# Attention for the next half woven into a feed-forward network: where TensorE's visits to the attention stand

## The chip, the cores and the metric

The kernel runs on one core of a Trainium2 chip. The metric is the device time of one execution in microseconds. The median of three runs of the kernel before is 941.1 us (940.64 to 941.63).

## What is computed

Attention over 8 batches, 8 heads, 576 positions and 64 dimensions, four heads with a plain window of 32 keys and four with 32 keys at a stride of 4; its result goes through a feed-forward network of 512 and 2048 with an exact GELU.

```python
def _attn_ref(q, k, v):
    scores = scale * np.matmul(q, k.transpose(0, 1, 3, 2))
    mask_plain = (rel >= 0) & (rel < window)
    mask_dil = (rel >= 0) & (rel < window * dilation) & (rel % dilation == 0)
    ...
    scores = np.where(masks[None, :, :, :], scores, -1000000000.0)
    scores = scores - np.max(scores, axis=-1, keepdims=True)
    attn = np.exp(scores)
    attn = attn / (np.sum(attn, axis=-1, keepdims=True) + 1e-09)
    return np.matmul(attn, v)

def _moe_ref(x, w_in, w_out):
    h = x @ w_in
    g = 0.5 * h * (1.0 + erf(h * inv_sqrt2))
    return g @ w_out
```

## The kernel before, in words

The 8 batches are cut into 16 halves of 288 positions, c = 0 to 15. For each half the heads form four pairs, p = 0 and 1 with the plain window and p = 2 and 3 with the dilated one. The network of a half takes 384 matrix products of 128 by 128 by 288 on TensorE: 16 hidden blocks of 12 each (`ffn_h`, L470) and four output blocks of 16 times 3 each (`ffn_o`, L484).

Halves 0 to 2 and the first two networks are ordered by a planner (`Plan`, up to L624). The change doesn't touch them. From the network of half 2 on (L667) the order is written out by hand: while TensorE works on the network of half c-1, the attention of half c is woven in. A step has a place, counted in units of 12 products: place f stands behind hidden block f, place 16 + 4d + f/4 behind the f-th part of output block d, and 32 is the start of the next network. `upto` (L661) emits each step when the loop comes to its place. Since every engine works through its instructions in the order in which they are emitted, a place sets where a step stands in the queue of each engine that it uses.

For half c, with places counted from the start of the network of half c-1:

- `load` (place -6, that is, place 26 of the network before): one DMA for each pair, issued on SP, for its queries and keys (`raw_qk`, L276). `all_v` (place 2): four DMAs for the values (L283).
- `scores_of` (A_SC, L629): TensorE multiplies queries with keys, 36 small products (64 rows by 32 columns, L328) for a plain pair, and for a dilated one 48 where c is even or 3, and 32 otherwise. Pairs 0 and 1 share one PSUM tile `ps_a`, pairs 2 and 3 the next; there are two such tiles in a ring that the later products share. Pairs 0 and 1 stand at place 3, pairs 2 and 3 at place 9.
- `lowest` (A_SC too, L340): VectorE adds the mask and finds the maximum, two or three steps a pair.
- `softmax` (places 16.25 to 17, L349): ScalarE's exponentials.
- `norm` and `turn` (places 18.5, 20, 21.5 and 23.25, L370 to L394): VectorE divides and transposes.
- `av_of` (A_X, L640): TensorE multiplies with v, as many small products (64 by 64, L429) as the scores had, into a `px_a` tile of the same ring. Pairs 0 and 1 stand at place 22.5, pairs 2 and 3 at place 27.
- `xout` (A_X too): ScalarE casts the product to the high part `xh` (L456), VectorE takes the low part `xl` (L459). Both feed the next network.

So TensorE leaves the network four times in a half for what is called a visit below: two for scores, two for products with v. There are 13 woven halves (3 to 15), so 52 visits. Around them stand the network's own steps: behind each hidden block a GELU and a cast on ScalarE (L474, L477) and a subtraction on VectorE (L479), behind each output block a copy on VectorE (L185) and a store that SP issues (L509).

Of the kernel before, what the change touches and what calls it, by code (L numbers as in the profile page):

```python
# [138 lines left out]
def attn_ffn(ctx: ExitStack, tc: tile.TileContext, qk_p, qk_d, qk_w, qk_r, v_p0, v_d0, v_p, v_d, w_in, w_out, outT):  # L139
# [129 lines left out]
    def load(s):  # L269

        yield {"DMA": 1.0 if s.plain else 1.2}
        if s.c < 2 or not s.plain:
            s.raw = wo.tile([P, 2 * DM], F32, tag="wo", name="raw_qk")
        else:
            s.raw = work.tile([P, HALF + KW], F32, tag="raw", name="raw_qk", bufs=5)
        nc.sync.dma_start(s.raw[:, 0:s.n], s.src)  # L276
# [8 lines left out]
    def all_v(c):  # L285

        v = work.tile([P, NPAIR, NU, 2, 2 * D], F32, tag="big", name="v_all", bufs=1)
        for s in xs[c]:
            s.v = v[:, s.p]
            yield from load_v(s)  # L290
# [4 lines left out]
    def rows_of(s, u):  # L295
        g = groups(s, u)
        return slice(32 * g[0], 32 * g[-1] + 32)
# [5 lines left out]
    def mask_of(s, u):  # L303
        k = ANY if s.c % 2 or u else PLAIN0 if s.plain else DILATED0
        return masks[rows_of(s, u), k]

    def scores(s, banks=None):

        yield {"PE": 0.75}
        if banks is None:  # L310
            s.sc = [ps_m.tile([P, 512], F32, tag="m", name="ps_sc")[:, 0:2 * KB * NU] for _ in range(2)]
        else:
            s.sc = [banks[:, h, s.p % 2 * 2 * KB * NU:(s.p % 2 + 1) * 2 * KB * NU] for h in range(2)]
        for u in range(s.nu):
            for r in groups(s, u):
                if s.across:
                    q0 = (4 * u + r if u < 2 else 8) * KB
                    k0 = HALF + q0
                elif s.split:

                    q0 = r * s.nq + u * KB
                    k0 = DIL * s.nq + r * s.nk + (u - (s.c % 2 == 0)) * KB
                else:
                    q0 = r * s.nq + u * KB
                    k0 = HALF + r * s.nk + u * KB
                for h in range(2):
                    x = s.raw[h * D:(h + 1) * D]
                    nc.tensor.matmul(s.sc[h][32 * r:32 * r + 32, u * 2 * KB:(u + 1) * 2 * KB], x[:, q0:q0 + 32],  # L328
                                     x[:, k0:k0 + 2 * KB], start=True, stop=True)

    def lowest(s, u):

        yield {"DVE": 0.28}
        if u == 0:
            s.sm = work.tile([P, 2 * NU, 2 * KB], F32, tag="sm", name="sm", bufs=5)
            s.st = work.tile([P, 2, 2 * NU], F32, tag="st", name="st", bufs=5)
        cols, rs = slice(u * 2 * KB, (u + 1) * 2 * KB), rows_of(s, u)
        for h in range(2):
            i = 2 * u + h
            nc.vector.tensor_tensor_reduce(  # L340
                out=s.sm[rs, i], in0=s.sc[h][rs, cols], in1=mask_of(s, u), scale=-SCALE,
                scalar=3.0e38, op0=ALU.add, op1=ALU.min, accum_out=s.st[rs, 0, i:i + 1])

    def softmax(s, u):
        yield {"ACT/exp": 0.66}
        for i in (2 * u, 2 * u + 1):
            rs = rows_of(s, u)
            t = s.sm[rs, i]
            nc.scalar.activation(t, t, AF.Exp, bias=s.st[rs, 0, i:i + 1], scale=-1.0, accum_out=s.st[rs, 1, i:i + 1])  # L349
# [16 lines left out]
    def norm(s):  # L366
        for rs, u0, u1 in parts(s):
            t, st = s.sm[rs, 2 * u0:2 * u1], s.st[rs, 1, 2 * u0:2 * u1]
            yield {"DVE": 0.07}
            nc.vector.tensor_scalar_add(st, st, EPS)  # L370
            yield {"DVE": 0.1}
            nc.vector.reciprocal(st, st)
            if s.c in (1, 2):
                yield {"Pool": 2.2}
                for i in range(2 * NU):
                    nc.gpsimd.tensor_scalar(t[:, i], t[:, i], st[:, i:i + 1], 1.0, op0=ALU.mult, op1=ALU.mult)  # L376
                continue
            yield {"DVE": 0.47}
            nc.vector.tensor_mul(t, t, st.unsqueeze(2).broadcast_to((rs.stop - rs.start, 2 * (u1 - u0), 2 * KB)))  # L379

    def turn(s):

        s.t = work.tile([P, 2 * NU, 2, KB], F32, tag="sm", name="turned", bufs=5)
        for rs, u0, u1 in parts(s):
            yield {"DVE": 0.5}
            i = slice(2 * u0, 2 * u1)
            nc.vector.transpose(s.t[rs, i].rearrange("p i j b -> p (i j b)"), s.sm[rs, i].rearrange("p i k -> p (i k)"))  # L389
            if s.c >= 2:  # L390
                for r in groups(s, u0):
                    yield {"DVE": 0.3}
                    to, j = r ^ 1, 1 - r % 2
                    nc.vector.transpose(s.t[32 * to:32 * to + 32, i, r % 2],  # L394
                                        s.sm[32 * r:32 * r + 32, i, j * KB:(j + 1) * KB])
# [37 lines left out]
    def xout(s):  # L433
        for i, (px, r0, r1) in enumerate(s.px):
            yield {"ACT": 0.46 if len(s.px) == 1 else 0.34}
            if i == 0:
                if s.c == 1:
                    s.x = s.of["x"][:, s.p, 0], s.of["x"][:, s.p, 1]
                else:
                    s.x = tuple(xpool.tile([P, HALF], F32R, tag=n, name=n) for n in ("xh", "xl"))  # L440
            if s.across:
                two = [x[:, 0:8 * KB].rearrange("p (u r b) -> p r u b", u=2, r=4) for x in s.x]
                put = [(px[:, :, 0:2 * KB].rearrange("p r (u b) -> p r u b", u=2), two),
                       (px[:, s.nine, 2 * KB:], [x[:, 8 * KB:] for x in s.x])]
            elif s.split:
                xs_ = [x.rearrange("p (i r) -> p r i", r=DIL) for x in s.x]
                if s.c % 2:
                    put = [(s.kept, [x[:, :, 0:QD - QR] for x in xs_]), (px, [x[:, :, QD - QR:] for x in xs_])]
                else:
                    put = [(px[:, :, 0:QD], xs_)]  # L450
                    nc.scalar.copy(s.kept, px[:, :, QD:])
            else:
                put = [(px, [x.rearrange("p (r i) -> p r i" if s.plain else "p (i r) -> p r i", r=s.nr)[:, r0:r1]
                             for x in s.x])]
            for y, (h, l) in put:
                nc.scalar.copy(h, y)  # L456
            yield {"DVE": 0.48 if len(s.px) == 1 else 0.3}
            for y, (h, l) in put:
                nc.vector.tensor_sub(l, y, h)  # L459
# [166 lines left out]

    A_LOAD, A_V, A_SC, A_X = -6, 2, (3, 3, 9, 9), (22.5, 22.5, 27, 27)  # L629
    A_E, A_N = (16.25, 16.5, 16.75, 17), (18.5, 20, 21.5, 23.25)  # L630
    ps_a = upper_banks("ps_a", 2)
    steps, banks = [], {}
# [1 line left out]
    def scores_of(s):  # L634
        if s.p % 2 == 0:
            banks["s"] = ps_a.tile([P, 2, 512], F32, tag="a", name="ps_a")
        yield from scores(s, banks["s"])

    def av_of(s):
        if s.p % 2 == 0:  # L640
            banks["x"] = ps_a.tile([P, 2, 512], F32, tag="a", name="px_a")
        yield from av(s, banks["x"])

    for c in range(3, NCH):
        def add(at, rank, gen, c=c):
            steps.append((2 * NF * (c - 1) + at, rank, len(steps), gen))
        add(A_V, 0, all_v(c))
        for p, s in enumerate(xs[c]):
            add(A_LOAD, 0, load(s))
            add(A_SC[p], 1, scores_of(s))  # L650
            for u in range(s.nu):
                add(A_SC[p], 2, lowest(s, u))
                add(A_E[p], 3, softmax(s, u))
            add(A_N[p], 4, norm(s))
            add(A_N[p], 5, turn(s))
            add(A_X[p], 6, av_of(s))
            add(A_X[p], 7, xout(s))
    steps.sort(key=lambda t: t[:3])
    at = 0

# [107 lines left out]
```

## Time and profile before

| | us |
|---|---|
| median of three runs | 941.1 |
| the profiled execution, its own time | 942.59 |
| its span, first to last instruction | 940.8 |
| TensorE busy with products | 914.6 |
| VectorE busy | 491.5 |
| ScalarE busy | 429.7 |
| mean granted clock of TensorE | 0.994 |

The prediction is made from views of this one execution. The chain of waits is followed back from the last instruction; its rows give a start, a duration, an engine, the tile written, a line and a count. Rows of the timeline give start, duration, engine, line, operation, tiles, shapes and count. Rows of windows give, for a stretch, the busy time of each engine with the number of its instructions in brackets, then the granted clock, the share of the DMA engines and GB/s. PE is TensorE's product, PEld its weight load; every product has one of each.

### The profile page before, as it was taken

The page shows a single profiled execution, that of the slowest core. Times are in us where ns is not written, and L with a number is a line of the kernel's source. Part 1 is how long each engine was busy: PE and PEld are TensorE (multiplying, and loading weights), DVE is VectorE, ACT ScalarE, POOL GpSimd, SP SyncE. Part 2 cuts the span into 40 slices and gives each one's busy share as a digit, 9 for nine tenths or more (in the row PEclk, how much of TensorE's full clock was granted, in tenths as well). Part 3 has the DMA queues.
Part 4 walks back from the last instruction along what each step waited for, and adds up shares of the span by engine and source line. Part 5 has one row for each costly group of instructions (what it writes and reads, how often), then busy time and mean ns, then how long its engine had stood idle before and what let it go on. Part 6 is the DMA issues. An engine that isn't in the chain of part 4 may idle for free.

```text
span 940.8 us, 26805 instructions
## 1 busy us (share of the span) xinstructions
PE 914.6 (97%) x11248; PEld 896.5 (95%) x11248; DVE 491.5 (52%) x1921; ACT 429.7 (46%) x1374; POOL 20.9 (2%) x64
## 2 busy tenths in 40 slices
PE   4599999999999999999999999999999999999998
PEld 3499999999999999999999999999999999999998
DVE  7889984363634546354363635436354354635420
ACT  6534453544536245452534536244363624546240
POOL 1400011000000000000000000000000000000000
PEclk9979999999999999999999999999999999999999
DMA  9978233122040311304022040302204022030000
GB/s 333 403 273 277 90 120 112 38 80 75 8 137 2 111 44 31 115 8 147 2 71 75 8 147 8 106 34 72 84 8 138 2 86 69 9 137 8 21 1 26
DMA packets 34985, 82.75 MB, mean 88 GB/s; under 512 B 3888, under 2 KB 12080, under 8 KB 34864
## 3 DMA queue, kind: packets, MB, share of 16 engines
q1 hardware_dynamic: 34864, 81.04, 25.1%
q8 instruction: 88, 1.44, 0.7%
q14 instruction: 33, 0.27, 0.1%
HBM read 71.59 MB, written 9.44 MB: 86 GB/s over the span
## 4 chain that ended last, share of the span: by engine, by line
PE 96%; DMA 2%; issue 1%; DVE 1%; SPq 0%; ACT 0%; DVEq 0%
PE ps_h L470 44%; PE ps_o L484 44%; PE px_a L429 4%; PE ps_a L328 3%; DMA mid_w<-w_in 1%; DMA raw_qk<-qk_d 1%; PE px L413 1%; PE ps_sc L328 0%; PE px L429 0%; ACT sm L349 0%; SPq L283 0%; SPq L276 0%; DVE cv L205 0%; DVE sm L340 0%; DVE xl L459 0%
## 5 line engine op out<-in xcount | busy, mean ns | idle before, releaser
L484 PE MATMUL ps_o<-g,wout 128*128 128x288 f32 x3072 | 420.3, 296 | 0.0
L484 PEld LDWEIGHTS ps_o<-g,wout 128*128 128x128 f32 x3072 | 409.9, 188 | 1.1
L470 PE MATMUL ps_h<-xh,win 128*128 128x288 f32 x1920 | 390.6, 299 | 0.0
L470 PEld LDWEIGHTS ps_h<-xh,win 128*128 128x128 f32 x1920 | 309.9, 190 | 2.9 <-issue 0.3
L470 PE MATMUL ps_h<-xl,win 128*128 128x288 f32 x960 | 285.1, 297 | 0.0
L479 DVE TENSOR_TENSOR g<-gf,g 128x288 fp32r<-128x288 f32 x256 | 117.1, 457 | 262.0 <-ACT g L477 261.8
L474 ACT ACTIVATE gf<-ps_h 128x288 f32<-128x288 f32 x256 | 105.3, 411 | 301.1 <-PE ps_h L470 300.4
L470 PEld LDWEIGHTS ps_h<-xl,win 128*128 128x128 f32 x960 | 182.1, 190 | 0.0
L349 ACT ACTIVATE sm<-sm,st 128x64 f32<-128x64 f32 (+2 forms) x336 | 112.2, 335 | 11.5 <-DVE st L340 10.4
L477 ACT CAST g<-gf 128x288 fp32r<-128x288 f32 x256 | 111.0, 433 | 7.9
L394 DVE STREAM_TRANSPOSE turned<-sm 32x128 f32<-32x128 f32 (+2 forms) x248 | 78.1, 315 | 6.2
L456 ACT CAST xh<-px_a 128x256 fp32r<-128x256 f32 (+2 forms) x78 | 27.5, 387 | 99.5 <-PE px_a L429 61.4
L185 DVE COPY o_sb<-ps_o 128x288 f32<-128x288 f32 x58 | 26.4, 456 | 85.9 <-PE ps_o L484 85.1
L349 ACT ACTIVATION_READ_ACCUMULATOR sm<-sm,st 128x1 f32 (+2 forms) x336 | 62.7, 186 | 0.0
L459 DVE TENSOR_TENSOR xl<-px_a,xh 128x256 fp32r<-128x256 f32 (+2 forms) x78 | 29.0, 399 | 37.4 <-ACT xh L456 37.0
L340 DVE CUSTOM_DVE_ANT_0 sm<-ps_a,masks 128x64 f32<-128x64 f32 (+1 forms) x288 | 44.5, 216 | 0.6
L389 DVE STREAM_TRANSPOSE turned<-sm 128x256 f32<-128x256 f32 (+2 forms) x90 | 39.5, 439 | 9.2 <-POOL sm L376 4.4
L429 PEld LDWEIGHTS px_a<-turned,v_all 64*64 64x64 f32 x1992 | 32.7, 135 | 4.2 <-issue 4.2
L429 PE MATMUL px_a<-turned,v_all 64*64 64x32 f32 (+2 forms) x1992 | 35.5, 219 | 0.0
L379 DVE TENSOR_TENSOR sm<-sm,st 128x256 f32<-128x256 f32 (+2 forms) x82 | 33.5, 408 | 2.8
L370 DVE TENSOR_SCALAR st<-st 128x4 f32<-128x4 f32 (+2 forms) x90 | 14.3, 160 | 31.0 <-ACT sm L349 30.1
L328 PE MATMUL ps_sc<-raw_qk 64*32 64x64 f32 x504 | 12.4, 300 | 17.1 <-issue 7.5
(43 smaller groups left out, 398.8 us busy)
## 6 DMA issues: line engine op xcount, KB each, us to landing
v_all<-v_p SPq DMA_DIRECT2D x28, 384.0 KB, 4.0
v_all<-v_d SPq DMA_DIRECT2D x28, 384.0 KB, 5.4
raw_qk<-qk_p SPq DMA_DIRECT2D x32, 304.0 KB, 4.2
outT<-o_sb SPq DMA_DIRECT2D x64, 144.0 KB, 1.8
raw_w<-w_in SPq DMA_DIRECT2D x16, 512.0 KB, 5.4
raw_w<-w_out SPq DMA_DIRECT2D x16, 512.0 KB, 5.6
mid_w<-w_out SPq DMA_DIRECT2D x10, 511.5 KB, 7.6
raw_qk<-qk_w SPq DMA_DIRECT2D x12, 384.0 KB, 5.4
```

Source lines behind the costliest of these rows:

```text
L328: nc.tensor.matmul(s.sc[h][32 * r:32 * r + 32, u * 2 * KB:(u + 1) * 2 * KB], x[:, q0:q0 + 32], x[:, k0:k0 + 2 * KB], start=True, stop=True)
L340: nc.vector.tensor_tensor_reduce(out=s.sm[rs, i], in0=s.sc[h][rs, cols], in1=mask_of(s, u), scale=-SCALE, scalar=3.0e38, op0=ALU.add, op1= ...
L349: nc.scalar.activation(t, t, AF.Exp, bias=s.st[rs, 0, i:i + 1], scale=-1.0, accum_out=s.st[rs, 1, i:i + 1])
L379: nc.vector.tensor_mul(t, t, st.unsqueeze(2).broadcast_to((rs.stop - rs.start, 2 * (u1 - u0), 2 * KB)))
L389: nc.vector.transpose(s.t[rs, i].rearrange("p i j b -> p (i j b)"), s.sm[rs, i].rearrange("p i k -> p (i k)"))
L394: nc.vector.transpose(s.t[32 * to:32 * to + 32, i, r % 2], s.sm[32 * r:32 * r + 32, i, j * KB:(j + 1) * KB])
L429: nc.tensor.matmul(px[h * D:(h + 1) * D, r - r0, u * KB:u * KB + b], s.v[rows, u, j, h * D:(h + 1) * D], s.t[rows, 2 * u + h, j, 0:b], sta ...
L470: nc.tensor.matmul(ps, wins[f][:, t, cc * P:(cc + 1) * P], xx, start=(n == 0), stop=(n == 3 * NC - 1))
L474: nc.scalar.activation(gf, ps, AF.Gelu)
L477: nc.scalar.copy(g[:, 0], gf)
L479: nc.vector.tensor_sub(g[:, 1], gf, g[:, 0])
L484: nc.tensor.matmul(ps, wouts[f][:, t, d * P:(d + 1) * P], gs[f][:, u], start=(f == 0 and n == 0), stop=(f == NF - 1 and n == 2))
```

## The change

The scores of all four pairs of a half stand at one place, which is chosen for each half. In nine of the 13 halves the products with v of all four pairs also stand at one place; in the other four (`None`) they stay at 22.5 and 27. The steps of `lowest` no longer stand at the place of the scores, but half a place apart behind it. Nothing is computed in another way, and no DMA moves.

```diff
-    A_LOAD, A_V, A_SC, A_X = -6, 2, (3, 3, 9, 9), (22.5, 22.5, 27, 27)
+    A_LOAD, A_V = -6, 2
+    A_SC = (3, 4, 2, 6, 3, 8, 3, 3, 4, 3, 6, 4, 3)
+    A_X = (None, None, 28.25, 27, 27, 27, 27, 28.25, 27, None, 27, None, 28.5)
+    PARTS = 22.5, 22.5, 27, 27
...
             add(A_LOAD, 0, load(s))
-            add(A_SC[p], 1, scores_of(s))
+            sc, x = A_SC[c - 3], A_X[c - 3] or PARTS[p]
+            add(sc, 1, scores_of(s))
             for u in range(s.nu):
-                add(A_SC[p], 2, lowest(s, u))
+                add(sc + (3 * p + u) / 2, 2, lowest(s, u))
                 add(A_E[p], 3, softmax(s, u))
             add(A_N[p], 4, norm(s))
             add(A_N[p], 5, turn(s))
-            add(A_X[p], 6, av_of(s))
-            add(A_X[p], 7, xout(s))
+            add(x, 6, av_of(s))
+            add(x, 7, xout(s))
```

The entries of A_SC and A_X belong to halves 3 to 15 in turn.

## The prediction

> **What bounds the kernel now.** I read the page first: which engine has no idle time (busy time, share of the span and instructions), and what the chain that ended last is made of.
>
> ```profile
> PE 914.6 (97%) x11248; PEld 896.5 (95%) x11248; DVE 491.5 (52%) x1921; ACT 429.7 (46%) x1374; POOL 20.9 (2%) x64
> ...
> PE 96%; DMA 2%; issue 1%; DVE 1%; SPq 0%; ACT 0%; DVEq 0%
> ```
>
> TensorE is the whole chain. A change is worth what it takes from TensorE's own sequence, plus or minus the waits that it makes there. So next come the pieces of the chain of waits (start, us, what) over one woven half, the one in which the attention of half 7 is made.
>
> ```profile
> 381.67 6.37 PE ps_h L470 x48
> 388.04 0.91 PE ps_a L328 x60
> 388.95 9.75 PE ps_h L470 x72
> 398.70 0.79 PE ps_a L328 x53
> 399.49 9.76 PE ps_h L470 x72
> ```
>
> The pieces join: TensorE goes from the network to a visit for scores and back, with no wait between; the two visits for v follow in the same way, and the next half starts at 437.37, 55.70 us after this one. What a visit costs beyond its products follows from whole stretches (columns: length, then busy time and count of PE, PEld, DVE, ACT, POOL, clock, DMA share, GB/s).
>
> ```profile
> 381.67:437.37 55.70, 55.70 (x659) 54.79 (x658) 26.36 (x110) 25.37 (x82) 0.00 (x0) 1.00 0.20 66
> 437.37:493.90 56.53, 56.53 (x723) 55.62 (x722) 27.80 (x116) 26.94 (x90) 0.00 (x0) 1.00 0.19 61
> 886.59:937.48 50.89, 50.88 (x384) 50.65 (x383) 9.16 (x20) 13.50 (x32) 0.00 (x0) 1.00 0.04 13
> ```
>
> The clock is whole. The third row is the last network, which has nothing woven in: 384 products in 50.89 us, 0.1325 us each. So four visits cost 55.70 - 50.89 = 4.81 us with 272 small products (an odd half: 72 + 64 for the scores, as many with v) and 56.53 - 50.89 = 5.64 us with 336 (an even one). The difference gives 0.83 / 64 = 13.0 ns a small product. There remain 4.81 - 272 x 0.0130 = 1.27 us for four visits, **0.32 us a visit** that doesn't depend on how many products it has. The scores alone, from the timeline, two visits of 64 and 96 products with their neighbours:
>
> ```profile
> 398.41 0.29 PE L470 MATMUL ps_h<-xl,win 128*128 128x288 f32 x1
> 398.63 0.86 PE L328 MATMUL ps_a<-raw_qk 64*32 64x64 f32 x64
> 399.42 0.53 PE L470 MATMUL ps_h<-xh,win 128*128 128x288 f32 x2
> ```
> ```profile
> 454.11 0.29 PE L470 MATMUL ps_h<-xl,win 128*128 128x288 f32 x1
> 454.33 1.20 PE L328 MATMUL ps_a<-raw_qk 64*32 64x64 f32 x96
> 455.46 0.54 PE L470 MATMUL ps_h<-xh,win 128*128 128x288 f32 x2
> ```
>
> From the last product of the network to the next it takes 1.01 and 1.35 us: 0.34 / 32 = 10.6 ns a product. Less the 0.13 us that this step takes undisturbed, 1.01 - 0.13 - 64 x 0.0106 = 0.20 us, and behind it the first two products take 0.53 where an undisturbed two take 0.29 + 0.13 = 0.42: together 0.31 us. With 0.32 as the mean of all, a visit for v has 0.33. Half of it is seen directly, as idle time before the first weight load of each visit, 0.16 us, 26 times for each kind:
>
> ```profile
> PEld ps_a L328 <- issue: 4.2, 26, 0.2
> PEld px_a L429 <- issue: 4.2, 26, 0.2
> ```
>
> There are 52 of them, one a visit, though every visit holds two pairs: the cost goes with the change between network and attention, not with a pair.
>
> **The change, part by part.** Removed: one of two score visits in each of 13 halves, and one of two visits for v in the nine halves with one place (5 to 11, 13 and 15). That is 22 visits x 0.32 = 7.0 us; by the ends 22 x 0.30 = 6.6 and 22 x 0.34 = 7.5 (a hundredth beyond each kind's value). The products themselves stay.
>
> The scores of pairs 2 and 3 now come up to seven places earlier (9 to 2; a place is 12 x 0.1325 = 1.6 us). They need `raw_qk`. SP's issues around half 7's end, and their landing (KB each, us to landing):
>
> ```profile
> 429.65 0.85 SPq L276 DMA_DIRECT2D raw_qk<-qk_w  x2
> ```
> ```profile
> raw_qk<-qk_w SPq DMA_DIRECT2D x2, 384.0 KB, 6.6
> ```
>
> They land near 430.1 + 6.6 = 436.7; the earliest score visit (place 2) would be at 437.37 + 3 x 1.6 = 442.1, so 5 us of cover. SP's queue is not reordered. Half 3 is the exception: its loads can't be issued six places ahead, since the planner's part ends only there.
>
> ```profile
> 158.11 0.90 SPq L276 DMA_DIRECT2D raw_qk<-qk_d  x2
> ```
> ```profile
> raw_qk<-qk_d SPq DMA_DIRECT2D x1, 364.0 KB, 5.7
> ```
>
> The last load, issued at 158.6, lands 5.7 us later, at 164.3 (the second row is that load alone). Merged at place 3, the visit starts at 162.5 (as the first one does now; a row below ends there) and reaches pair 3 after 72 + 48 products, 120 x 0.0106 = 1.3 us, at 163.8: a new wait of **0.5 us**, once. What is behind it on TensorE is the network itself. The ends are 0 (a faster landing) and 0.8 (a late signal).
>
> The PSUM ring has two tiles. The merged scores need both free at once, so `xout` of all pairs must be over; but the next network needs that earlier still, at place 32. The merged products ask for the last transposed pair at place 27 or later; what VectorE and ScalarE do before:
>
> ```profile
> 423.60 0.52 DVE L459 TENSOR_TENSOR xl<-px_a,xh 128x256 fp32r<-128x256 f32 x2
> 424.65 0.52 DVE L459 TENSOR_TENSOR xl<-px_a,xh 128x256 fp32r<-128x256 f32 x2 [0.53 <-ACT xh L456]
> ...
> 426.44 1.29 DVE L394 STREAM_TRANSPOSE turned<-sm 32x128 f32<-32x128 f32 x4
> ```
> ```profile
> 429.70 0.50 ACT L456 CAST xh<-px_a 128x192 fp32r<-128x192 f32 x1 [4.83 <-PE px_a L429]
> ...
> 430.76 0.50 ACT L456 CAST xh<-px_a 128x192 fp32r<-128x192 f32 x1 [0.39 <-DVE xl L459]
> ```
>
> Pair 3's transposes end at 427.73 behind the two subtractions of pairs 0 and 1, which now move behind them: some 1.5 us sooner, 426.2. TensorE now reaches place 27 at 437.37 - 57 x 0.1325 - (64 x 0.0130 + 0.32) = 428.7; with the visit gone from 22.5 (72 x 0.0130 + 0.32 = 1.3 us) at 427.4, and pair 3 after 104 products, 1.4 us later. Cover: 428.8 - 426.2 = 2.6 us. ScalarE takes 431.26 - 429.70 = 1.56 us for the casts of two pairs, so at most 3.1 for four, and VectorE's last subtraction follows; the latest place, 28.5, leaves 39 products of the network, 39 x 0.1325 = 5.2 us, plus the visit itself. Nothing is late. Behind VectorE's four subtractions the copy of output block 2 waits, and SP's store behind that, at most 3 us; PSUM's bank of it is next needed two places into the next network. VectorE's `lowest`, spread out, delays the network's own subtraction less than now. So these edits cost nothing, and would cost the part of the 5.2 us that is exceeded.
>
> **The instruction stream.** A merged visit is 272 or 336 instructions of TensorE in 2 us (each product has a weight load), and instructions come by DMA. The page's row for it, and the chain, early in the kernel:
>
> ```profile
> q8 instruction: 88, 1.44, 0.7%
> ```
> ```profile
> 25.48 2.48 issue
> ...
> 44.21 2.98 issue
> ```
>
> 1.44 MB / 88 = 16.4 KB a packet, and 22,496 products and weight loads / 88 = 256 instructions each. The two rows are stops of TensorE for which no engine is named. They stand at equal counts of instructions:
>
> ```profile
> 15.10:21.80 6.70, 3.44 (x127) 2.58 (x127) 5.77 (x30) 3.94 (x23) 0.00 (x0) 1.00 1.03 366
> 21.80:27.90 6.10, 2.87 (x127) 2.30 (x127) 5.63 (x31) 5.44 (x26) 4.59 (x9) 1.00 1.03 398
> ```
>
> Each stretch ends with a stop and holds 254 products and loads (semaphore instructions aren't counted): one block of 256. So a block takes 6.1 to 6.7 us to come after the one before was begun, with the DMA engines full (share 1.03), and a burst of small products that runs through a block sooner stops TensorE.
>
> Where do the edges of the blocks fall in the merged visits?
>
> ```profile
> 47.18:162.54 115.36, 115.35 (x1081) 113.64 (x1080) 93.51 (x239) 50.00 (x112) 6.93 (x24) 0.96 0.52 171
> 437.00:445.00 8.00, 8.00 (x126) 7.75 (x126) 2.15 (x5) 3.38 (x8) 0.00 (x0) 1.00 0.65 217
> ```
>
> From the edge at 47.18 to half 3's first score there are 2161 instructions and some 10 semaphores: 2161 + 10 = 8 x 256 + 123. Its 336 run from 123 to 459 of a 512: one edge inside, and 53 instructions of the network, 3.5 us, before the next. Behind the edge come 203 / 2 x 0.0106 = 1.1 us of scores and that, 4.6 us in all, and the sequencer has passed the edge earlier by as much as it works ahead of the array. Counting on in this way, all merged visits but the last (half 15's products, 249 to 521) end before 512. With a lead of 33 instructions (an estimate: 2.2 us of network; the rows show none), the shortest times from edge to edge are 3.8 to 5.1 us, in seven places. If a fetch takes 4.5 us, 1.0 us is lost in all, at 5.5 us 5.8, at 6.4 us 15.2, and below 3.7 us nothing. The stops had a DMA share of 1.03, a woven half has 0.20, and 0.65 for 8 us while the values load; I take a fetch of about 4 us and **0.2 us**, and keep 0 and 15 as ends.
>
> [...]
>
> Sum: 7.0 - 0.5 - 0.2 = **6.3 us** saved. Against the profiled execution, 942.59 - 6.3 = 936.3; the median of the runs before is 1.5 below that execution, so 941.1 - 6.3 = **934.8 us**.
>
> **Rivals.**
> (1) Some fetches are late, by 1 to 5 us in sum (a fetch of 4.5 to 5.4 us): 936 to 940. For it: place 2 to 4 falls into the loads of v, with a share of 0.65. Against: no such stop in the woven stage of before.
> (2) The fixed cost doesn't go away: it is paid between pairs inside a visit too, now hidden, or the queue runs dry in a visit of 168 products. Then 941 + 0.5 for half 3. Against: 96 products run at the same 10.6 ns as 64.
> (3) One of the covers is short, say the casts behind place 28.5 by 1 us, in three halves: 938.
> (4) Slower: a fetch takes as long as early on, 6.4 us, and 14 edges are late for 15.2 us: 941.1 - 6.5 + 15.2 = 949.8. It decides from a fetch of 5.6 us on. Against: the DMA engines' share of 0.20.
>
> **How the numbers follow.** A measurement of this kernel tells 0.2%, 1.9 us, from no change. Forecast (933.2 to 936): 0.70. Rival 1: 0.12, of which 0.03 within 0.2%. Rival 2: 0.06, within. Rival 3: 0.04, faster. Rival 4: 0.08, slower. So faster 0.70 + 0.09 + 0.04 = 0.83, same 0.09, slower 0.08. The range goes from 941.1 - 7.5 - 0.6 (spread of the runs) = 933.0 up to 938.8, which takes in most of rivals 1 and 3.
>
> **What would show it.** Rows of PEld with 0.16 us of idle time on "issue": 13 for `ps_a` and 17 for `px_a` in place of 26 and 26; an odd merged half 55.70 - 0.64 = 55.06 us and an even one 55.89. A wait for `raw_qk` of about 0.5 us at 163.8. Stops on "issue" of over 0.2 us behind 120 us would show rivals 1 and 4, and a wait of L470 for `xh` or `xl` rival 3. What would make it wrong above all is the place of the edges, since a shift by 64 instructions puts several visits over two of them.

## The result, and the profile after

The changed kernel takes 936.36 us (median of six runs, 935.39 to 937.32) against 941.37: a ratio of 0.9948, 95% interval 0.9935 to 0.9961. That is 5.0 us, where 6.3 were predicted; 936.36 lies inside the predicted range of 933.0 to 938.8. Measured a second time beside other kernels it took 935.46 us, ratio 0.9941 (0.9928 to 0.9953).

First the page of the changed kernel, then the waits of TensorE's weight loads (what waited, on what: us in total, times, longest):

```profile
PE 903.9 (97%) x11248; PEld 890.7 (95%) x11248; DVE 491.4 (53%) x1921; ACT 428.6 (46%) x1374; POOL 20.9 (2%) x64
...
PE 95%; DMA 2%; issue 2%; SPq 0%; ACT 0%; DVE 0%; DVEq 0%
```
```profile
PEld px_a L429 <- issue: 2.8, 17, 0.2
...
PEld ps_a L328 <- issue: 2.1, 13, 0.2
...
PEld ps_o L484 <- issue: 1.3, 1, 1.3
PEld ps_h L470 <- issue: 1.2, 1, 1.2
```

TensorE still is the chain. The small waits of 0.16 us ahead of a visit number 17 and 13, in place of 26 and 26, as predicted. New are the last two rows, one wait each of over 1 us for nothing that has a name. The windows of the changed kernel say in which halves (from the start of the network of a half to that of the next; the attention of halves 3 to 7 is made in them):

```profile
154.95:212.97 58.02, 56.87 (x722) 55.76 (x721) 27.34 (x115) 28.21 (x90) 0.00 (x0) 1.00 0.25 87
212.97:269.20 56.23, 56.23 (x723) 55.57 (x722) 27.80 (x116) 26.92 (x90) 0.00 (x0) 1.00 0.19 61
269.20:324.15 54.95, 54.95 (x659) 54.51 (x657) 26.36 (x110) 25.24 (x82) 0.00 (x0) 1.00 0.20 67
324.15:379.93 55.78, 55.78 (x723) 55.33 (x722) 27.88 (x116) 26.85 (x90) 0.00 (x0) 1.00 0.19 62
379.93:436.21 56.28, 55.23 (x658) 54.56 (x657) 26.26 (x110) 25.23 (x82) 0.00 (x0) 1.00 0.20 65
```

Before, an even half took 56.53 and an odd one 55.70. Half 4 has only its scores merged and takes 0.30 us less. Half 5 (odd) and half 6 (even) have both merged and take 0.75 us less each, more than the predicted 0.64. Against that, half 3 is longer by 1.4 us than before (58.02 against 56.58) and half 7 by 0.6, and in both TensorE's busy time is over 1 us short of the length. The timeline and the chain of waits show where:

```profile
161.41 1.61 PE L328 MATMUL ps_a<-raw_qk 64*32 64x64 f32 x120
163.20 0.72 PE L328 MATMUL ps_a<-raw_qk 64*32 64x64 f32 x48 [0.19 <-DMA raw_qk<-qk_d]
```
```profile
163.93 3.65 PE ps_h L470 x26
167.58 0.96 issue
168.54 15.93 PE ps_h L470 x118
```
```profile
425.22 2.10 PE px_a L429 x136
427.32 1.93 PE ps_o L484 x13
429.25 1.04 issue
430.30 1.72 PE ps_o L484 x11
```

Half 3's visit waits for its last queries and keys, as was expected. Then, 26 products of the network behind the visit, TensorE stops for 0.96 us. A product and its weight load are two instructions: 52, where the prediction had counted 53 to the next edge of an instruction block. The other stop comes behind half 7's products. Between the ends of the two stops lies this many instructions (counts of PE and PEld):

```profile
168.50:430.25 261.75, 260.71 (x3186) 258.08 (x3186) 131.91 (x550) 125.03 (x420) 0.00 (x0) 1.00 0.18 60
```

3186 + 3186 = 6372, and the trace records 28 semaphore instructions on TensorE's queue between them: 6400 = 25 x 256. From 167 to 429 us, up to the second stop, the DMA view has as many packets of instructions:

```profile
q8 instruction: 25, 0.41, 0.7%
```

So the two stops stand at the same place of a block of 256, at its edge.

### The profile page after: what moved, and what is told of

Its sections match the earlier page's. It is cut to its first block, busy times and chain, and to the rows that moved or that the text cites. A ratio compares the mean times of both kernels' runs of the same rounds, so it can differ in the third digit from the quotient of the medians.

```text
span 934.6 us, 26805 instructions
## 1 busy us (share of the span) xinstructions
PE 903.9 (97%) x11248; PEld 890.7 (95%) x11248; DVE 491.4 (53%) x1921; ACT 428.6 (46%) x1374; POOL 20.9 (2%) x64
## 4 chain that ended last, share of the span: by engine, by line
PE 95%; DMA 2%; issue 2%; SPq 0%; ACT 0%; DVE 0%; DVEq 0%
PE ps_o L484 44%; PE ps_h L470 44%; PE px_a L429 3%; PE ps_a L328 2%; DMA raw_qk<-qk_d 1%; DMA mid_w<-w_in 1%; PE px L413 1%; PE ps_sc L328 1%; PE px L429 0%; SPq L276 0%; ACT sm L349 0%; SPq L283 0%; DVE xl L459 0%; ACT xh L456 0%; DVE o_sb L185 0%
## 5 line engine op out<-in xcount | busy, mean ns | idle before, releaser
L340 DVE CUSTOM_DVE_ANT_0 sm<-ps_a,masks 128x64 f32<-128x64 f32 (+1 forms) x288 | 48.9, 219 | 0.6
L429 PE MATMUL px_a<-turned,v_all 64*64 64x32 f32 (+2 forms) x1992 | 32.8, 218 | 0.0
```

Of the source, the lines that this page charges most:

```text
L340: nc.vector.tensor_tensor_reduce(out=s.sm[rs, i], in0=s.sc[h][rs, cols], in1=mask_of(s, u), scale=-SCALE, scalar=3.0e38, op0=ALU.add, op1= ...
L429: nc.tensor.matmul(px[h * D:(h + 1) * D, r - r0, u * KB:u * KB + b], s.v[rows, u, j, h * D:(h + 1) * D], s.t[rows, 2 * u + h, j, 0:b], sta ...
```

## The experiments

The theory to test: (a) a visit costs 0.3 to 0.45 us whatever it holds; (b) TensorE stops where it gets through a block before the next one has come; (c) the block comes late because its fetch stands behind the loads that run then. The rival to (a) was a smaller gain a visit, 5.0 / 22 = 0.23 us; to (b) and (c), that the stops are chance, come with the length of a visit, or that a fetch always takes long. Every edit below is against the changed kernel.

### Both stops away (e4_mended)

```diff
-    A_SC = (3, 4, 2, ...
-    A_X = (None, None, 28.25, 27, 27, 27, ...
+    A_SC = (10, 4, 2, ...
+    A_X = (None, None, 28.25, 27, None, 27, ...
```

> The changed kernel with half 3's scores at place 10 (in place of 3) and half 7's products with v split again (22.5 and 27). Theory (a visit of TensorE costs about 0.33 us for scores and 0.43 us for v whatever it holds; the changed kernel loses 0.5 us to a load of half 3 and 1.0 to 1.3 us at each of two edges of instruction blocks): both stops and the wait are gone, half 3 takes 58.0 - 1.8 = 56.2 us, half 7 takes 56.3 - 1.3 + 0.4 = 55.4 us, in all 2.7 us less than the changed kernel: 933.7 us, within 933.2 to 934.3. Rival (the gain of a visit is only 5.0 / 22 = 0.23 us, and the two stops are chance): 0.23 us more than the changed kernel for the visit that comes back, and stops somewhere else: 936 to 937 us.

933.63 us, ratio 0.9921 (0.9907 to 0.9935). The windows of halves 3 and 7 are, to a hundredth or two, the lengths that were expected, and TensorE is busy all through them:

```profile
154.55:210.76 56.21, 56.21 (x723) 55.57 (x722) 27.33 (x115) 28.23 (x90) 0.00 (x0) 1.00 0.27 90
377.80:433.20 55.40, 55.40 (x658) 54.75 (x657) 26.34 (x110) 25.41 (x82) 0.00 (x0) 1.00 0.20 66
```

So the stops and the wait come from the visits that were moved (half 3) or split (half 7), and half 7's stop was worth more than the visit that it gives back.

### Scores alone, products alone (e1_scores_only, e2_products_only)

```diff
-    A_X = (None, None, 28.25, 27, 27, 27, 27, 28.25, 27, None, 27, None, 28.5)
+    A_X = (None,) * 13
```

> Only the scores merged, at the changed kernel's places; all products with v at 22.5 and 27 as before. Theory: 13 visits x 0.33 = 4.3 us saved, half 3's wait and stop (1.8 us) stay, half 7's stop goes, since its long visit is gone: 941.1 - 4.3 + 1.8 = 938.6 us; each half from 4 to 15 is 0.33 us shorter than before. Rival (0.23 us a visit): each half 0.23 us shorter, 941.1 - 3.0 + 1.8 = 939.9 us.

```diff
-            sc, x = A_SC[c - 3], A_X[c - 3] or PARTS[p]
+            sc, x = (3, 3, 9, 9)[p], A_X[c - 3] or PARTS[p]
...
-                add(sc + (3 * p + u) / 2, 2, lowest(s, u))
+                add(sc, 2, lowest(s, u))
```

> Only the products with v merged, in the nine halves and at the places of the changed kernel; scores at 3 and 9 as before. Theory: nine visits x 0.43 = 3.9 us saved; half 7's visit has the same place in its block as in the changed kernel, so its stop of about 1 to 1.3 us stays, half 3 has none: 941.1 - 3.9 + 1.2 = 938.4 us; the other eight halves are 0.43 us shorter each. Rival (0.23 us a visit): 0.23 us each, 941.1 - 2.1 + 1.2 = 940.2 us. If a visit for v costs no more than one for scores: 0.33 each, 939.3 us.

937.95 us, ratio 0.9966 (0.9954 to 0.9979), and 938.86 us, ratio 0.9975 (0.9963 to 0.9986). The totals hardly tell the theories apart; the windows of halves 4 and 5 with the scores alone, and then of 5 and 6 with the products alone, do:

```profile
213.27:269.47 56.20, 56.20 (x722) 55.54 (x721) 27.78 (x116) 26.90 (x90) 0.00 (x0) 1.00 0.19 62
269.47:324.87 55.40, 55.40 (x659) 54.75 (x658) 26.35 (x110) 25.41 (x82) 0.00 (x0) 1.00 0.20 66
```
```profile
267.21:322.54 55.33, 55.33 (x659) 54.63 (x658) 26.36 (x110) 25.25 (x82) 0.00 (x0) 1.00 0.20 66
322.54:378.63 56.09, 56.09 (x722) 55.38 (x721) 27.87 (x116) 26.84 (x90) 0.00 (x0) 1.00 0.19 62
```

A merged score visit takes 56.53 - 56.20 = 0.33 us off an even half and 55.70 - 55.40 = 0.30 off an odd one. Merged products take 0.37 off the odd and 0.44 off the even half. 0.23 is out. With the scores alone half 3 took 57.23 us; its wait for queries and keys was there (0.5 us), but its stop, which was expected to stay, was not. With the products alone half 7 didn't stop in the profiled execution, though its stop was expected to stay (its window is 55.30); the times of this kernel spread from 935.98 to 941.25, so that execution need not be typical.

### Twice the visits (e5_four)

```diff
+            sc, x = (3, 5, 9, 11)[p], (22.5, 24, 27, 28)[p]
```

> Each pair by itself: scores of the four pairs at 3, 5, 9 and 11, products with v at 22.5, 24, 27 and 28, so 104 visits in place of 52 of the kernel before. Theory: 26 more visits for scores x 0.33 and 26 more for v x 0.33 to 0.43: 17.2 to 19.8 us more, 958 to 961 us; no visit holds an edge and a long burst, so no stop on instructions. Rival (the cost belongs to a pair, or a visit costs 0.23 us): 941 or 953 us.

979.75 us, ratio 1.0404 (1.0388 to 1.0421): 38.7 us more, twice what was expected. The waits of TensorE and the windows of halves 4 and 5:

```profile
PE px_a L429 <- DVE xl L459: 14.6, 13, 1.4
```
```profile
214.23:273.70 59.47, 58.09 (x723) 56.19 (x721) 27.80 (x116) 26.90 (x90) 0.00 (x0) 1.00 0.17 58
273.70:331.58 57.88, 57.05 (x659) 55.17 (x658) 26.37 (x110) 25.40 (x82) 0.00 (x0) 1.00 0.19 63
```

The waits stand ahead of the second of the four visits for v, one in each half. In half 4, first TensorE's visit, then what VectorE does:

```profile
258.47 0.77 PE L429 MATMUL px_a<-turned,v_all 64*64 64x32 f32 x36 [1.38 <-DVE xl L459]
```
```profile
256.37 1.52 DVE L394 STREAM_TRANSPOSE turned<-sm 32x192 f32<-32x192 f32 x4
257.90 0.52 DVE L459 TENSOR_TENSOR xl<-px_a,xh 128x256 fp32r<-128x256 f32 x2
```

Pair 1's products go into the tile `px_a` that pair 0's subtraction still reads, and that subtraction stands behind pair 2's transposes on VectorE. While both pairs were made in one visit, nothing stood between them. Without that idle time (59.47 - 58.09 and 57.88 - 57.05), four more visits cost 58.09 - 56.53 = 1.56 and 57.05 - 55.70 = 1.35 us, 0.39 and 0.34 each. That agrees with (a), and a cost that goes with a pair, which would have left the time at 941 us, is out. As a total the run is spoiled by the wait, which was not expected. Halves 6 and 14 took 1.5 us more than the other even ones. In each the granted clock fell to about half for 3.4 us, which costs that much; what made it fall isn't known:

```profile
377.00:380.40 3.40, 3.40 (x17) 3.40 (x16) 2.72 (x8) 0.09 (x2) 0.00 (x0) 0.53 0.08 26
```

### No count (e3_uniform)

```diff
+    A_SC = (3,) * 13
+    A_X = (27,) * 13
```

> One visit for scores at place 3 and one for v at place 27 in every half, without a count: 26 visits fewer than before. Theory (TensorE stops where it gets through a block of 256 instructions before the next one has come, 3.6 us after the edge in quiet traffic and up to 6.4 us while loads run): the visits save 13 x 0.33 + 13 x 0.43 = 9.9 us, half 3's load costs 0.5, and the visits that would run over two edges stop: by the count of places the scores of halves 6 and 14 and the products of halves 3, 5 and 10 do, with 2.6 us in all if every fetch is quiet and up to 30 if every one is slow; I expect 5 to 12 us in 5 to 10 stops, 936.5 to 943.5 us, above the mended kernel's 933.6. Rival (the place in the block doesn't matter, only traffic at halves 3 and 7): 941.1 - 9.9 + 0.5 + 2.3 = 934 us, with stops in those two halves alone.

942.7 us, ratio 1.0018 (1.0005 to 1.0031). All 26 visits are saved and nothing is gained. A piece of its chain of waits, halves 12 and 13:

```profile
705.46 2.34 PE px_a L429 x150
707.80 1.92 issue
709.72 0.53 PE px_a L429 x18
710.25 9.26 PE ps_o L484 x57
719.51 6.37 PE ps_h L470 x48
725.88 1.53 PE ps_a L328 x95
727.41 1.55 issue
728.96 0.30 PE ps_a L328 x4
```

There are seven stops of 0.4 to 1.9 us, 8.6 us in all: in the scores of halves 6, 8 and 13 and the products of half 12 in the midst of the visit, at its second edge, and behind a visit in halves 3, 4 and 14. Counted with the semaphore instructions, they lie 9, 7, 11, 25, 2 and 9 blocks of 256 apart. The expected number and size (5 to 12 us) hold; which halves, hardly: of the expected scores of 6 and 14 and products of 3, 5 and 10, only half 6's scores stopped. The rival, stops in halves 3 and 7 alone, is out. Nor does such a stop need loads: the DMA engines stand idle in the one at 727.41 (first row below). Not all that half 12 lost is the stop: behind it 57 products take 9.26 us where they take 7.73 elsewhere, since there too the granted clock was about half for 3.4 us (second row):

```profile
727.40:728.96 1.56, 0.01 (x2) 0.00 (x1) 0.17 (x4) 0.00 (x0) 0.00 (x0) 1.00 0.00 0
711.40:714.85 3.45, 3.45 (x16) 3.45 (x16) 1.47 (x3) 2.11 (x3) 0.00 (x0) 0.53 0.26 97
```

### Half 7's stop (e7_c7_26, e8_c7_2775, e6_load_later, e11_after_again)

In turn: half 7's products at 26, at 27.75, the loads of queries and keys at place -4 in place of -6, and the changed kernel once more.

> The changed kernel with half 7's products at place 26 in place of 27: 24 instructions of the network, 1.6 us, are moved behind the visit, between it and the next edge. Theory: half 7's stop of 1.0 us is gone, the half takes 55.7 - 0.73 = 55.0 us; half 3 is as in the changed kernel; 936.4 - 1.3 = 935.1 us. Rival (the stop comes from the length of the visit or from the loads alone): it stays, 936.4 us.

> The changed kernel with half 7's products at place 27.75: 18 instructions, 1.2 us, fewer between the visit and the next edge. Theory: the stop behind the visit is 1.2 us longer, 2.2 us, and half 7 takes 57.5 us; if the fetch happens to be quiet, the stop is under 0.5 us. Rival (length or loads alone): 1.0 us as in the changed kernel, 56.3 us.

> The changed kernel with the loads of queries and keys two places (3.2 us) later, at -4: behind half 7's products in place of ahead of them. Theory (the fetch of a block is slow because it waits behind these loads): half 7's stop is gone, the half takes 55.0 us; half 3, whose loads don't move, is unchanged; 935.1 us, unless the later loads slow a fetch in a score visit at place 2 to 4. Rival (a fetch always takes about 6 us): half 7's stop stays, 936.4 us.

> The changed kernel once more, as it is, beside the two others. Theory: half 3's stop and wait come every time, half 7's only where the fetch starts late, since a run with half 7's products at 27.75 and less cover hardly showed it: 935 to 936.5 us, about 2.3 us over the mended kernel. Rival (half 7's stop is in every execution): half 7 takes 56.3 us again.

| half 7's products | half 7, us | median, us | ratio to before |
|---|---|---|---|
| at 27 (first profile) | 56.28 | 936.36 | 0.9948 (0.9935 to 0.9961) |
| at 27 (again) | 55.88 | 935.46 | 0.9941 (0.9928 to 0.9953) |
| at 26 | 54.98 | 935.32 | 0.9942 (0.9922 to 0.9962) |
| at 27.75 | 55.08 | 935.11 (one run) | |
| at 27, loads later | 54.97 | 934.85 | 0.9939 (0.992 to 0.9958) |

The windows tell the stop; the totals can't, at 1 us. The stop wasn't chance, but its length varies: 1.04 us on the chain in the first profile, 0.58 in the second (half 7 at 55.88, between what the theory and its rival gave), and 0.74 in each of the two runs of the next section, which leave half 7 as it is. At 26 it is gone, as expected, and with the loads later it is gone, which the length of the visit or a fetch that is always slow doesn't explain. At 27.75 my expectation of a longer stop was wrong. SP's issues show why. First the changed kernel, then the one with 27.75, then the later loads:

```profile
425.28 0.92 SPq L276 DMA_DIRECT2D raw_qk<-qk_p  x2
```
```profile
425.24 2.55 SPq L276 DMA_DIRECT2D raw_qk<-qk_p  x2
```
```profile
431.14 0.92 SPq L276 DMA_DIRECT2D raw_qk<-qk_p  x2
```

From the start of the visit to the stop there are 2 x 136 + 2 x 13 = 298 products and weight loads and three semaphore instructions, so the edge before lies 301 - 256 = 45 instructions into the visit. In the changed kernel the loads start with the visit (425.2), and the DMA view has the block's one packet in 428.0 to 428.1, some 2.5 us behind that edge. With 27.75 the edge lies 27 instructions into the visit, and the packet starts in 425.6 to 425.7, ahead of the visit's own start at 426.40, with TensorE's products still those of the network, and the fetch got away with the loads barely begun (the first is issued at 425.24). With the later loads the packet starts in 426.4 to 426.5. The DMA engines' traffic at that edge in the changed kernel:

```profile
425.00:428.00 3.00, 3.00 (x143) 2.82 (x142) 0.52 (x2) 0.94 (x5) 0.00 (x0) 1.00 0.73 180
```

A late start isn't all: in the second profile of the changed kernel the packet starts at 426.3, beside the loads, and takes 2.1 us, where it takes 1.0 with the later loads. By these runs, what sets this stop is whether the fetch runs beside the loads. The run at 26 can't tell the cover behind the visit from that: there the packet starts in 424.0 to 424.1, and the loads only at 424.4.

### Half 3's stop (e10_v_later, e12_v_by_act)

```diff
-        add(A_V, 0, all_v(c))
+        add(14 if c == 3 else A_V, 0, all_v(c))
```

> The changed kernel with half 3's four loads of v at place 14 in place of 2, so that they no longer run when its scores are made. Theory (the fetch of the block waits behind these loads): the stop behind the scores of half 3, 0.5 to 1.0 us so far, is gone, and half 3 takes 57.5 - 0.5 to 1.0 = 56.5 to 56.9 us; the wait for its last queries and keys stays or shrinks. 1 us less than the changed kernel. Rival (a fetch takes 6 us whatever runs): the stop stays, 57.4 us or more.

This edit did nothing of what it was meant to. SP's issues in that run:

```profile
157.39 0.86 SPq L283 DMA_DIRECT2D v_all<-v_p  x2
```

A place orders SP's queue, but nothing in that queue waits for TensorE at this point, so the loads of v still go out at 157.4. Half 3 took 57.55 us and the kernel 934.98, ratio 0.993 (0.9917 to 0.9944); on the question it says nothing. The next run issues them from ScalarE, whose queue does wait:

```diff
-        nc.sync.dma_start(s.v[rows], s.vsrc[rows])
+        (nc.scalar if s.c == 3 else nc.sync).dma_start(s.v[rows], s.vsrc[rows])
...
+        add(6 if c == 3 else A_V, 0, all_v(c))
```

> The changed kernel with half 3's four loads of v issued by ScalarE behind its seventh GELU of that half (some 10 us later than now), in place of SP, which doesn't wait for the place and issues them at once. Theory (the fetch of the block and the last queries and keys wait behind these loads): the stop behind half 3's scores is gone, its wait for queries and keys too or down to 0.2 us; half 3 takes 56.2 to 56.5 us in place of 57.3, about 1 us less in all, and half 7's stop of 0.9 to 1.0 us stays. Rival (that fetch takes 6 us whatever runs): the stop of 0.5 to 1.0 us stays and half 3 takes 57 us or more.

934.56 us, ratio 0.9924 (0.991 to 0.9938). The loads of v now start behind a GELU, at 169.1, after the visit:

```profile
169.09 0.86 ACTq L283 DMA_DIRECT2D v_all<-v_p  x2
```

Its windows: the traffic around half 3's scores, and halves 3 and 7; then what is left of TensorE's waits in all woven halves:

```profile
163.00:167.00 4.00, 4.00 (x80) 3.91 (x74) 0.97 (x9) 0.84 (x2) 0.00 (x0) 1.00 0.04 8
```
```profile
155.11:211.40 56.29, 56.29 (x722) 55.64 (x721) 27.27 (x115) 28.12 (x90) 0.00 (x0) 1.00 0.27 90
378.47:434.49 56.02, 55.28 (x658) 54.60 (x657) 26.25 (x110) 25.26 (x82) 0.00 (x0) 1.00 0.20 65
```
```profile
PE ps_o L484 <- issue: 0.7, 1, 0.7
```

Half 3's stop and its wait for queries and keys are both gone with TensorE's instructions the same, and half 7's stop, which this edit doesn't touch, is there. In the eight other profiles with half 3's scores merged at place 3 and its loads of v in place, how wait and stop share the loss varies, but half 3 took 57.2 to 58.0 us in every one, against 56.29 here. The changed kernel has the traffic in its windows:

```profile
158.00:166.00 8.00, 7.81 (x211) 7.33 (x210) 2.12 (x8) 3.57 (x10) 0.00 (x0) 1.00 0.94 343
166.00:168.50 2.50, 1.58 (x12) 1.35 (x11) 1.26 (x10) 1.45 (x4) 0.00 (x0) 1.00 0.07 18
```

There, the DMA view has no packet of q8 in 162 to 166 and one in 166 to 167: it starts when the loads end. With the loads of v away one starts in 163 to 164. So (c) holds for half 3 by the run that moves the loads, and for half 7 by the one that moves its loads.

### A version that beats both (e9_best)

```diff
+    A_SC = (10, 4, 2, 6, 3, 8, 3, 3, 4, 3, 6, 4, 3)
+    A_X = (28.25, None, 28.25, 27, 26, 27, 27, 28.25, 27, None, 27, 26.25, 28.5)
```

> Half 3's scores at place 10, half 7's products at 26, and two more halves with one visit for v: half 3 at 28.25 and half 14 at 26.25, at places whose count leaves a full block's time between edges. Theory: no stop and no wait; halves 3 and 14 take 55.8 us (56.57 - 0.35 - 0.43), half 7 takes 55.0; against the mended kernel three visits fewer, 933.6 - 1.3 = 932.3 us. Rival (gains are used up; the casts behind 28.25 or the transposes ahead of 26.25 come late): a wait of L470 for the low part in half 3, or of the product for the transposed pair in half 14, and 933.6 us or more.

931.75 us, ratio 0.9894 (0.988 to 0.9909). Halves 3 and 14:

```profile
154.51:210.30 55.79, 55.79 (x722) 55.34 (x721) 27.54 (x115) 28.13 (x90) 0.00 (x0) 1.00 0.27 90
765.04:820.85 55.81, 55.81 (x723) 55.35 (x721) 27.87 (x116) 26.85 (x90) 0.00 (x0) 1.00 0.19 62
```

Half 7 takes 54.97 us. No stop and no wait of a product in any woven half, and 9.5 us less than before.

## Why the prediction was right in its range and short of its sum

- **TensorE is the chain, and a visit costs time whatever it holds.** Right. Halves of the same size differ by the visits alone, and twice the visits cost 0.34 to 0.39 us each.
- **22 visits x 0.32 = 7.0 us.** The mechanism was right, the term too small. From one network's start to the next, a merged score visit is worth 0.33 us (mean of halves 4 to 15 with the scores alone) and a merged visit for v 0.43 (mean of the nine halves with the products alone): 13 x 0.33 + 9 x 0.43 = 8.2 us. The products with v are the ones that were low (0.33 predicted): the step took from the even and odd halves a cost that doesn't grow with the number of products, and merging took away somewhat more than that. What the rest is wasn't tried.
- **Half 3's load, 0.5 us.** Right for the first profile: a wait for `raw_qk` there, named so by the profile. With it the visit takes 2.52 us (161.41 to 163.93), and 1.98 with the loads of v moved away. In two other profiles (e7, e11) the wait didn't show and the stop came alone.
- **Transposes, casts, PSUM ring: nothing late.** Right: no wait of the network for `xh` or `xl`, and none of the products for their transposes, up to place 28.5.
- **Fetches late: 0.2 us.** This is the step that failed. It was the first rival, a fetch of more than 4 us, and it came at two edges: 0.96 and 1.04 us on the chain, with what is lost around a stop some 1.3 us of each half's length, 2.6 in all. An estimate of the fetch, from the visits' rates: in half 3 TensorE passed the edge, 132 instructions into the visit, at about 161.41 + 66 x 0.0106 = 162.1 and went on behind the stop at 168.54, 6.4 us; in half 7 from 425.6 to 430.30, 4.7 us. For the uniform kernel's stop at 727.41, with no traffic in it, the same estimate gives 3.0 us (3.6 was expected of quiet traffic), so a fetch of about 4 us was a fair guess, but not beside these loads. The prediction took the mean DMA share of a half, 0.20, where the share at those edges decides: 0.94 ahead of half 3's stop, 0.73 at half 7's edge. It quoted 0.65 for the loads of v and half 3's late loads, and didn't put the two beside the list of edges. Its lead of 33 instructions, for which it showed no row, does stand in the profile before: in the last network the packets of q8 start at 892.0 and 909.1, 35 and 33 instructions (2.3 and 2.2 us) ahead of TensorE's coming to the edge of its block.
- **The place of the edges.** Half 3's was right (53 instructions behind the visit predicted, 52 found). For half 15's products the count gave 249 to 521; with the semaphore instructions that the trace records it is 39 to 314. No merged visit of the changed kernel runs over two edges.
- **The sum, half by half.** Half 3 takes 58.02 in place of the 56.2 that it takes undisturbed, 1.8 us lost, 0.5 to the wait and 1.3 to the stop. Half 7 loses 1.3 us (56.28 against 54.97). Of 8.2 us from the visits 5.1 are left, and 5.1 is what the thirteen halves lost in the profiles: 730.34 us before (156.25 to 886.59), 725.27 after (155.11 to 880.38). The medians differ by 5.0. Another 1.1 us by which the two profiled executions differ lies ahead of half 3, in a part that the change doesn't touch. That the forecast of 6.3 came so near is in part luck: the visits gave 1.2 us more than predicted and the fetches took 2.4 more.
- **The slower rival.** Not here, since the places avoid a second edge. With uniform places the same mechanism, with some 1.5 us of a lower clock in the profiled execution, took all of the gain: 942.7 us.

## What to carry to other kernels

Where an engine issues instructions in bursts, count them: here stops on "issue" at equal counts (256) told that TensorE outran its instructions, and 24 instructions of slower work, moved from ahead of a burst to behind it, took the stop of 1.04 us away. Put such a burst, and above all the edge in it, where no large load is in flight, and look at the DMA share at that place (0.94 and 0.73 at the two stops) and not at its mean (0.20). A place in program order needn't delay a DMA: on SP, where nothing ahead of them waited, the loads of v went out at 157.4 in spite of place 14, and on ScalarE, behind a GELU, at 169.1; check the issue time before reading anything from such a run.

## What the runs showed of the hardware

- The long stops on "issue" in the woven halves stand multiples of 256 instructions of TensorE apart, 25 x 256 in the changed kernel and 2 to 25 x 256 in the uniform one, and in the changed kernel those 25 blocks came in 25 packets of q8, 16.4 KB each.
- The block's packet can start late behind loads: in the changed kernel for half 3 only when the share had fallen from 0.94 to 0.07, some 4 us behind the edge (166.1 against 162.1). In the network alone the edges cost nothing that shows: there one comes every 17 us (128 products of 0.1325 us), and the last network of the kernel before, with packets at 892.0 and 909.1, keeps TensorE busy for 50.88 of 50.89 us. In the bursts an edge cost up to 1.92 us (the uniform kernel).
- A change of TensorE between the network's products (128 by 128) and small ones costs 0.30 to 0.44 us, there and back: 0.30 and 0.33 for a visit for scores, 0.37 and 0.44 for one for v, 0.34 and 0.39 each with twice the visits. 0.16 us of it is idle time ahead of the visit's first weight load: 52 times in the kernel before and 30 times in the changed one, once a visit, and never between the pairs inside one. No run shows the cause: the shape of the products and the type of the operands (fp32r, then f32) change at the same places.
- The granted clock fell to 0.53 for some 3.4 us in the midst of a kernel, at a cost of 1.5 us: in two halves with four visits each for scores and v, and in one of the uniform kernel. Why isn't shown.
